# Sliding-window attention and a SMELU feed-forward network: from two stages over DRAM to one interleaved stream with transposed two-head scores

## The chip, the cores and the metric

The kernel runs on one core of one Trainium2 chip. The metric is the device time of one execution in microseconds (us). The runs of one kernel lie between 0.2% and 1.1% apart, lowest to highest. The engines are PE (matmul; weight loads counted apart), DVE (vector), ACT (activation), POOL (which here also issues most transfers) and SP. In the traces of this case each works through its own instructions in program order; run y2 below rests on this. PE leaves its results in PSUM, and the copy that takes one from there to SBUF, where the other tiles lie, is called an eviction.

## The reference

Attention over batch 8, 8 heads, 576 positions and head size 64, in which a query sees the keys at most 32 positions away; then a two-layer network on the 4608 tokens (512 to 2048 to 512) with the SMELU activation.

```
scores = q @ k.T / 8                       # per batch and head
attn   = softmax(where(|i - j| <= 32, scores, -1e9))
x      = (attn @ v), heads side by side     # 4608 x 512
h      = x @ w_in                           # 4608 x 2048
g      = h if h >= 1, 0 if h <= -1, else (h + 1)**2 / 4
out    = g @ w_out                          # 4608 x 512, fp32
```

## The kernel before

Attention goes head by head and by blocks of 128 queries. Scores have queries on the partitions, so the probabilities must be transposed on PE, in up to two chunks, before they meet v. Each chunk of v is a transfer of its own, and x goes out to DRAM, transposed.

```
for qs in qb_starts:                                    # 5 blocks per head
    nc.tensor.matmul(sc[:nq, :nk], qT[:, ds(qs, nq)], kT[:, ds(ks, nk)], ...)
    nc.vector.scalar_tensor_tensor(scs[:nq, :nk], sc[:nq, :nk], 0.125, mask[:nq, :nk], ...)
    nc.scalar.activation(pr[:nq, :nk], scs[:nq, :nk], AF.Exp, accum_out=sm[:nq])
    ...                                                 # reciprocal, scaling
    for ci in range(nchunk):
        nc.tensor.transpose(prT[:cw, :nq], pr[:nq, ds(ci * 128, cw)], ident[:nq, :nq])
        nc.scalar.copy(prTs[:cw, :nq], prT[:cw, :nq])
        nc.gpsimd.dma_start(out=vch[:cw], in_=v[b, h, ds(ks + ci * 128, cw), :])
        nc.tensor.matmul(ot[:, :nq], vch[:cw], prTs[:cw, :nq], ...)
    nc.scalar.copy(osb[:, :nq], ot[:, :nq])
    nc.gpsimd.dma_start(out=xT[ds(h * D, D), ds(b * S + qs, nq)], in_=osb[:, :nq])
```

The network follows when all of x is in DRAM. Its activation takes four DVE passes and one on ACT for each of 144 tiles of 128 x 512:

```
nc.vector.tensor_scalar(t1, hp, 1.0, 0.0, op0=ALU.add, op1=ALU.add)
nc.vector.tensor_scalar(t1, t1, 0.0, 2.0, op0=ALU.max, op1=ALU.min)
nc.scalar.activation(t2, t1, AF.Square, scale=0.5)
nc.vector.tensor_scalar(t1, hp, -1.0, 0.0, op0=ALU.add, op1=ALU.max)
nc.vector.tensor_add(gT[:, f, :], t2, t1)
```

The softmax here doesn't subtract the row's maximum and nothing guards it: scores larger than these inputs give would overflow.

## Time and profile before

The kernel before takes 1139.3 us (median). Its profile has two stages with different limits: attention (about 780 us), in which POOL is full of transfer issues, and the network (about 360 us), in which DVE is full of the activation's passes. The lines, and how each is read, are in the prediction. One digit of the busy map is the busy share of a slice in tenths; a group's line has the total of its busy time, the mean duration in ns, and after the bar the idle time just before its instructions with what ended it.

### The profile page before, as it was taken

Reading aid. Unit: us, or ns where it says so; the run is one execution under the profiler, and the core shown is the slowest. Engines: PE = TensorE matmul, PEld = TensorE weight load, DVE = VectorE, ACT = ScalarE, POOL = GpSimd, SP = SyncE. Lnnn points to the kernel's source line nnn. Section 1 sums busy time; section 2 is a strip of 40 time slices with the busy share of each in tenths; the row PEclk is TensorE's granted clock in tenths of the full one; section 3 lists DMA queues with packets and bytes.
Section 4 is the critical chain, followed back from the end, with each engine's and each line's share of the span. In section 5 each row is a group of like instructions: output and inputs, shape, how many; then the busy total and the mean of one; then the engine's idle time right before and its main releaser. Section 6 shows DMA issues by size and latency. Waiting matters only on the chain.

```text
span 1139.6 us, 13067 instructions
## 1 busy us (share of the span) xinstructions
PE 727.5 (64%) x2920; PEld 294.0 (26%) x2944; DVE 516.2 (45%) x1538; ACT 489.3 (43%) x2037; POOL 737.8 (65%) x1275
## 2 busy tenths in 40 slices
PE   3566656565654455555655655566888888888883
PEld 1222222222221122222222222222233232332321
DVE  1232222222222122222222222233999999999995
ACT  3545545454553345444454444543233323332332
POOL 6999999999998689899998998875001100110000
PEclk9999999999999999999999999999999999999998
DMA  6334434343435533333343333221001100110101
GB/s 92 30 29 32 31 29 31 30 30 29 31 28 65 73 43 30 28 28 30 27 31 27 30 30 26 23 20 13 20 37 55 56 19 38 55 56 19 38 37 38
DMA packets 158399, 40.24 MB, mean 35 GB/s; under 512 B 147184, under 2 KB 154352, under 8 KB 158320
## 3 DMA queue, kind: packets, MB, share of 16 engines
q0 software_dynamic: 158320, 39.40, 30.7%
q8 instruction: 23, 0.38, 0.1%
q14 instruction: 56, 0.46, 0.1%
HBM read 45.61 MB, written 14.16 MB: 52 GB/s over the span
## 4 chain that ended last, share of the span: by engine, by line
issue 40%; POOL 29%; DMA 16%; PE 8%; ACT 5%; DVE 2%; POOLq 0%; ACTq 0%; DVEq 0%
POOL vch L100 12%; DMA vch<-in_v_dram 11%; POOL nat L65 8%; POOL xT L105 7%; DMA nat<-in_q_dram 3%; PE ot L101 3%; PE prT L96 3%; ACT prTs L98 2%; ACT pr L86 2%; POOL out_dram L142 2%; PE sc L80 1%; DMA w_out<-in_moe_w_out_dram 1%; DVE scs L83 1%; PE tp L67 1%; ACT osb L104 1%
## 5 line engine op out<-in xcount | busy, mean ns | idle before, releaser
L100 POOL DMA_DIRECT2D vch<-in_v_dram x576 | 313.2, 547 | 31.9 <-PE ot L101 22.6
L89 DVE RECIPROCAL rs<-sm 128x1 f32<-128x1 f32 (+1 forms) x320 | 51.8, 162 | 546.2 <-ACT pr L86 546.1
L101 PE MATMUL ot<-prTs,vch 128*64 128x128 bf16 (+3 forms) x576 | 174.6, 307 | 101.8 <-DMA vch<-in_v_dram 96.9
L96 PE MATMUL prT<-ident,pr 128*128 128x128 bf16 (+3 forms) x576 | 154.8, 272 | 99.0 <-ACT prTs L98 91.9
L98 ACT COPY prTs<-prT 128x128 bf16<-128x128 bf16 (+3 forms) x576 | 142.8, 252 | 118.8 <-PE ot L101 115.0
L105 POOL DMA_DIRECT2D xT<-osb x320 | 174.5, 545 | 24.0 <-ACT prTs L98 12.9
L132 ACT ACTIVATE t<-t 128x512 f32<-128x512 f32 x144 | 90.7, 630 | 213.4 <-DVE t L130 213.4
L126 PE MATMUL hp<-xc,w_in 128*128 128x512 bf16 x563 | 147.9, 382 | 51.1 <-DVE t L133 50.4
L101 PEld LDWEIGHTS <-vch 128*64 128x64 bf16 (+3 forms) x576 | 72.4, 126 | 310.5 <-DMA vch<-in_v_dram 272.1
L138 PE MATMUL op<-w_out,gT 128*128 128x512 bf16 x565 | 147.9, 381 | 5.4 <-DVE gT L134 4.4
L80 PE MATMUL sc<-kT,qT 64*128 64x192 bf16 (+2 forms) x320 | 96.4, 304 | 81.5 <-DVE scs L83 73.4
L86 ACT ACTIVATE pr<-scs 128x192 bf16<-128x192 f32 (+2 forms) x320 | 109.3, 342 | 69.9 <-PE prT L96 62.0
L104 ACT CAST osb<-ot 64x128 bf16<-64x128 f32 (+1 forms) x320 | 78.1, 244 | 126.6 <-PE ot L101 115.6
L67 PE MATMUL tp<-ident,nat 128*128 128x128 bf16 (+1 forms) x320 | 86.7, 277 | 61.1 <-DMA nat<-in_q_dram 30.2
L65 POOL DMA_DIRECT2D nat<-in_q_dram x160 | 113.7, 711 | 15.6 <-DMA xT<-osb 10.9
L142 POOL DMA_DIRECT2D out_dram<-osb x36 | 19.5, 544 | 154.4 <-ACT osb L141 154.4
L65 POOL DMA_DIRECT2D nat<-in_k_dram x160 | 113.6, 711 | 8.0 <-PE tp L67 5.8
L121 POOL DMA_DIRECT2D xc<-xT x9 | 7.0, 776 | 160.2 <-PE hp L126 160.2
L129 DVE TENSOR_SCALAR t<-hp 128x512 f32<-128x512 f32 x144 | 99.6, 692 | 24.1 <-PE hp L126 9.1
L134 DVE TENSOR_TENSOR gT<-t,t 128x512 bf16<-128x512 f32 x144 | 98.6, 684 | 0.0
L133 DVE TENSOR_SCALAR t<-hp 128x512 f32<-128x512 f32 x144 | 98.1, 681 | 0.2 <-ACT t L132 0.2
L96 PEld LDWEIGHTS <-pr 128*128 128x128 bf16 (+3 forms) x576 | 69.9, 121 | 99.9 <-issue 60.3
(29 smaller groups left out, 582.0 us busy)
## 6 DMA issues: line engine op xcount, KB each, us to landing
out_dram<-osb POOLq DMA_DIRECT2D x36, 256.0 KB, 2.3
xc<-xT POOLq DMA_DIRECT2D x9, 512.0 KB, 4.3
nat<-in_k_dram POOLq DMA_DIRECT2D x128, 32.0 KB, 2.4
vch<-in_v_dram POOLq DMA_DIRECT2D x256, 16.0 KB, 2.1
nat<-in_q_dram POOLq DMA_DIRECT2D x128, 32.0 KB, 2.4
xT<-osb POOLq DMA_DIRECT2D x256, 16.0 KB, 1.8
vch<-in_v_dram POOLq DMA_DIRECT2D x192, 8.0 KB, 2.0
w_in<-in_moe_w_in_dram POOLq DMA_DIRECT2D x1, 2048.0 KB, 12.8
```

The costliest lines, as they stand in the source:

```text
L65: nc.gpsimd.dma_start(out=nat[:cw], in_=src[b, ds(2 * hp, 2), ds(cs, cw), :].rearrange("h s d -> s h d"))
L80: nc.tensor.matmul(sc[:nq, :nk], qT[:, ds(qs, nq)], kT[:, ds(ks, nk)], start=True, stop=True)
L86: nc.scalar.activation(pr[:nq, :nk], scs[:nq, :nk], AF.Exp, accum_out=sm[:nq])
L96: nc.tensor.transpose(prT[:cw, :nq], pr[:nq, ds(ci * 128, cw)], ident[:nq, :nq])
L98: nc.scalar.copy(prTs[:cw, :nq], prT[:cw, :nq])
L100: nc.gpsimd.dma_start(out=vch[:cw], in_=v[b, h, ds(ks + ci * 128, cw), :])
L101: nc.tensor.matmul(ot[:, :nq], vch[:cw], prTs[:cw, :nq], start=(ci == 0), stop=(ci == nchunk - 1))
L105: nc.gpsimd.dma_start(out=xT[ds(h * D, D), ds(b * S + qs, nq)], in_=osb[:, :nq])
L126: nc.tensor.matmul(hp, w_in[:, kk, ds(f * 128, 128)], xc[:, kk, :], start=(kk == 0), stop=(kk == 3))
L129: nc.vector.tensor_scalar(t1, hp, 1.0, 0.0, op0=ALU.add, op1=ALU.add)
L134: nc.vector.tensor_add(gT[:, f, :], t2, t1)
L138: nc.tensor.matmul(op, gT[:, f, ds(tt * 128, 128)], w_out[:, f, :], start=(f == 0), stop=(f == 15))
```

## The change

Its intent is to remove both limits at once. Attention and network become one stream of slots, in which every engine has some of each. Scores are computed transposed, keys on the partitions: a chunk of 64 keys of two heads, interleaved (partition 2s + h), is one weight tile of 128 columns, so no transpose of probabilities is needed. x stays on the chip. q, k and v come in few large transfers; because of their layout (position 9p + j on partition p), the transposed q and k must be spread over their rows when they leave PSUM. The SMELU is rewritten as max(h, -1) + (clamp(h, -1, 1)/2 - 1/2)^2, three passes.

The core of the diff, cut:

```diff
+    def tpose(m, t):                        # 5 or 4 transposes, then the eviction
+            if t < 2:                       # q, on DVE
+                nc.vector.tensor_copy(
+                    qT[m].rearrange("d g (p j) -> d j g p", j=NC)[:, j0:j1],
+                    ps[:, :n].rearrange("d j (g p) -> d j g p", g=2))
+            else:                           # k, on ACT, for 2 heads x 2 pairs
+                        nc.scalar.copy(
+                            kz[...][r].rearrange("d (p j t) -> d t p j", j=NC, t=2)[:, h, :, j0:j1],
+                            ps[r, :n].rearrange("d j (g p) -> d g p j", g=2)[:, g])
...
+            nc.tensor.matmul(ps[:, off:off + q1 - q0], kz[...][:, 128 * c:128 * c + 128],
+                             qT[m][:, gg, q0:q1], start=True, stop=True)
...
+            nc.scalar.activation(pt[i][:, seg], ps[:, :off], AF.Exp, scale=D ** -0.5)
+            nc.gpsimd.tensor_mul(pt[i][:, seg], pt[i][:, seg], maskp[:, seg])
...
+    for a in range(-1, OFF + 16 * (NBLK + 1)):      # the slots
+        if stt:
+            stt()                                    # final pass of the slot before
+            stt = None
+            ... 4 matmuls of the first product into hp ...
+            nc.vector.tensor_scalar(c1, hp, -1.0, 1.0, op0=ALU.max, op1=ALU.min)
+        ... normalisation, scores, exp ...
+            nc.scalar.activation(s1, c1, AF.Square, scale=0.5, bias=-0.5)
+            def stt(hp=hp, s1=s1, blk=blk, f=f):
+                nc.vector.scalar_tensor_tensor(gT[blk][:, f], hp, -1.0, s1, op0=ALU.max, op1=ALU.add)
+        ... 4 matmuls of the second product into op; after the last of 16 a copy on ACT, a store on SP ...
+        ... regrouping, transposes and evictions, or values and denominators ...
```

## The prediction

> **What bounds the kernel now.** I read the busy map of the page first, to see the stages.
> ```profile
> DVE  1232222222222122222222222233999999999995
> POOL 6999999999998689899998998875001100110000
> PEclk9999999999999999999999999999999999999998
> DMA  6334434343435533333343333221001100110101
> ```
> Each digit is a slice of 28.5 us. There are two kernels one after the other: attention for 27 slices (about 780 us) with POOL full, then the MoE for 13 (about 360 us) with DVE full. The TensorE clock is full throughout. The view of stages gives the busy time of each engine inside both:
> ```profile
> 30.00:340.00 310.00, 185.14 (x742) 79.01 (x741) 78.47 (x384) 160.04 (x764) 297.28 (x507) 1.00 0.40 30
> 800.00:1100.00 300.00, 251.40 (x1010) 89.85 (x1029) 285.90 (x514) 97.53 (x161) 22.72 (x39) 1.00 0.12 41
> ```
> The columns are PE, weight loads, DVE, ACT, POOL, then clock, DMA share, GB/s. POOL is busy 297 of 310 us, DVE 286 of 300 us. The chain that ended last agrees for attention: its first entries are
> ```profile
> POOL vch L100 12%; DMA vch<-in_v_dram 11%; POOL nat L65 8%; POOL xT L105 7%; DMA nat<-in_q_dram 3%; PE ot L101 3%; PE prT L96 3%; ACT prTs L98 2%; ACT pr L86 2%; POOL out_dram L142 2%; PE sc L80 1%; DMA w_out<-in_moe_w_out_dram 1%; DVE scs L83 1%; PE tp L67 1%; ACT osb L104 1%
> ```
> The groups, by form (busy us, mean ns), say what fills them:
> ```profile
> L100 POOL DMA_DIRECT2D vch<-in_v_dram x576 | 313.2, 547 | 31.9 <-PE ot L101 22.6 <-PE tp L67 4.8 <-PE prT L96 3.0
> L105 POOL DMA_DIRECT2D xT<-osb x320 | 174.5, 545 | 24.0 <-ACT prTs L98 12.9 <-ACT osb L104 7.6 <-ACT qT L68 2.8
> L129 DVE TENSOR_SCALAR t<-hp 128x512 f32<-128x512 f32 x144 | 99.6, 692 | 24.1 <-PE hp L126 9.1
> L134 DVE TENSOR_TENSOR gT<-t,t 128x512 bf16<-128x512 f32 x144 | 98.6, 684 | 0.0
> L132 ACT ACTIVATE t<-t 128x512 f32<-128x512 f32 x144 | 90.7, 630 | 213.4 <-DVE t L130 213.4
> L130 DVE TENSOR_SCALAR t<-t 128x512 f32<-128x512 f32 x144 | 60.4, 419 | 0.0
> L141 ACT COPY osb<-op 128x512 f32<-128x512 f32 x36 | 20.2, 586 | 17.9 <-DMA out_dram<-osb 13.1 <-PE op L138 4.8
> ```
> Attention: 1,216 issues (576 of v, 320 of x, 320 of q and k at 711 ns) = 313 + 175 + 227 = 715 us of POOL. MoE: four DVE passes, 0.692 + 0.419 + 0.681 + 0.684 = 2.48 us per feature tile, times 144 = 357 us. PE is not at its limit anywhere. What a matmul costs in a stream comes from the timeline:
> ```profile
> 906.92 1.02 PE L126 MATMUL hp<-xc,w_in 128*128 128x512 bf16 x4 [0.79 <-DVE t L133]
> 907.78 1.46 PE L138 MATMUL op<-w_out,gT 128*128 128x512 bf16 x6
> 303.31 0.29 PE L67 MATMUL tp<-ident,nat 128*128 128x128 bf16 x1
> 303.39 0.31 PE L96 MATMUL prT<-ident,pr 128*128 128x128 bf16 x1
> ```
> One lasts 0.38 us, but six take 1.46: (1.46 - 0.38)/5 = 0.216 us each. Two independent ones of 128 columns start 0.08 us apart.
>
> **What the Trainium skill says.** (1) "TensorE: Matmul & The Clock Gate", section "Back-to-back issue gap": 216 ns at N=512, and some 81 ns at N=128 with its weight load. Both agree with the lines above. (2) "VectorE: DVE Perf Modes", section on the TRN2 errata: (N+151)/0.96 ns for a one-per-cycle vector operation, which gives 691 ns at 512 (trace 692, 684); ACT (172+N)/1.2 from PSUM and (224+N)/1.2 from SBUF, 570 and 613 ns at 512 (trace 586, 630, 3% more). I use them for new widths. (3) "GPSIMD Engine Reference", section 3.1: a two-input POOL operation of 2048 elements takes 4497 ns. The trace has no such operation; estimate from that page for 352 to 384 elements: 0.9 us.
>
> **The change part by part.**
> Loads: q and k of four heads in 4 issues of 64 x 2 runs, v of a pair in 2 issues. x and the probabilities no longer move. 64 + 64 + 2 issues on POOL instead of 1,216, and out goes to SP. At 0.57 us per q/k issue (that of 128 runs) and about 0.85 per v issue (576 runs; estimate from 547 and 711 ns for 128 and 256), that is 91 us. POOL gets 96 mask multiplications at 0.9 = 86 us. Total some 180 us instead of 738.
> MoE: three passes, two on DVE (0.69 each from PSUM) and the square on ACT (0.63).
> Scores come out transposed, so the 576 probability transposes and their copies go; a 64-key chunk of two heads meets 96 or 128 queries, nine chunks per pair in groups of 352, 352 and 384 columns.
> The stream has slots: attention runs from slot 0 to 136 (four slots per head pair, first scores at 9), the first MoE products in slots 29 to 172, the second in 45 to 188. Engines keep program order, so a slot costs about its busiest engine. Per full slot:
> - PE: 8 matmuls x 0.216 = 1.73; per pair 9 scores, 9 transposes, 10 value products at 0.08 and 4 denominators at 0.115 = 2.70, a quarter of it 0.67. Sum 2.40.
> - DVE: 2 x 0.69 = 1.38; per eight slots 2 regroupings (0.6 each, estimate), q evictions of 640 and 512 elements (0.82 + 0.69) and 4 normalisations of 288 (0.46) = 4.55, an eighth 0.57. Sum 1.95.
> - ACT: 0.63 + a quarter of 0.586; per pair three exps (1.38), two Ln and Exp pairs (1.62), half of eight k evictions (1.53) = 4.53, a quarter 1.13. Sum 1.91.
> - POOL: per pair 3 x 0.9 + 2 x 0.85 + 2 x 0.57 = 5.5, a quarter 1.4.
> So PE becomes the bound at 2.40. Single PSUM buffers for scores, numerator, denominator and transposes cost little if a consumer finishes within the next slot; by my walk through the eight slot kinds the tightest, the exp after a k eviction, has some 0.4 us to spare. I take 2.5.
>
> Start: a transfer of POOL waits for the one eight issues before (the order of instructions shows these waits), and the first mask multiplications stand behind both weights in POOL's queue. Before, w_in took
> ```profile
> w_in<-in_moe_w_in_dram POOLq DMA_DIRECT2D x1, 2048.0 KB, 12.8
> ```
> and w_out 15.7 us. The page counts 147,184 packets under 512 B, nearly all in some 750 us of attention, so 61,000 in the 310 us above; at a DMA share of 0.40 that is 0.40 x 16 x 310 / 61,000 = 32 ns each. A v issue (576 such packets) then holds the 16 engines 1.15 us; a q/k issue of 147 KB at w_in's rate 0.7 us. To the landing of w_out: 16 x 0.7 + 16 x 1.15 + 10 + 10 + latency = about 53 us, when the third pair's masks (slot 17) can run.
>
> | slots | us each | sum | clock |
> |---|---|---|---|
> | to 16 | - | 53 | 53 |
> | 17-28, attention only (POOL 1.4 and latencies) | 1.65 | 20 | 73 |
> | 29-44, first product only (DVE 1.95) | 2.1 | 34 | 107 |
> | 45-136, full | 2.5 | 230 | 337 |
> | 137-172, MoE only (PE 1.73) | 1.76 | 63 | 400 |
> | 173-188, second product (4 x 0.216) | 0.87 | 14 | 414 |
> | last copy and store | - | 4 | 418 |
>
> **The rivals.**
> (A) ACT sets the full slots. For: slots with k evictions hold 2.6 to 2.9 us of ACT work, and these evictions read PSUM with a long stride, of which the trace has no example. At twice their estimate ACT has 2.3 us per slot, unevenly, and a late exp stalls the next scores: slot 2.75, total 441.
> (B) The waits between engines set it: scores, exp, mask, values, logarithm, product in a row through single buffers, as in attention before, where only the sum of "issue" and transfers explained the pace. Slot 3.2, total 482. Against: no link needs its answer within its own slot.
> (C) The start is hidden better, or small matmuls stream at 56 ns: slot 2.3, start 40: total 387.
> (D) The stream is DMA-bound: per pair 2 x 1.15 + 2 x 0.7 = 3.7 us of engines against 10 us of slots. Unlikely.
>
> **Range and chances.** The centre is 418; C and A give the nearer ends, and unknown operations (strided evictions, POOL product) mostly lengthen, so 393 to 470. Only a failure of the whole interleave would bring it near 1139: POOL's 715 and DVE's 357 us in series are gone whatever else happens. Faster 0.99.
>
> **What would show it.** PE should be densest from about 107 us on, 8 or 9 tenths and more, with hp and op matmuls as the last link of the chain, and DVE, ACT near 75 to 80% there. POOL's first mask product should stand behind weight transfers until about 40 us, with a gap to about 53. A full stretch of 16 slots should take 40 us, one of the MoE tail 28. Wrong if in 107 to 337 us PE waits for exp (A) or for a chain through all engines (B), if k evictions take over 0.5 us, or if the DVE evictions into strided places take over 0.9.

## The result, and the profile after

The changed kernel takes **473.3 us** (median of 4 runs, 471.9 to 474.0) against 1139.3, a ratio of 0.416 [0.415, 0.416]. A ratio is the mean time of one kernel's runs over that of the other's in the same rounds, so not quite the ratio of the medians quoted. The forecast said 418 within 393 to 470: the direction was clear, the size is 3 us outside the range and 55 us from the centre.

The busy map of the changed kernel (slices of 11.8 us) shows one stage instead of two, in which PE is the densest but not full:
```profile
PE   0135458567979787878787879787878999798976
DVE  5633556868777777777777777777776666666610
ACT  1057557575767666666666666666667743333320
POOL 8647586262717171717171726232223200000000
```
The chain of waits that ended last names PE only for parts of it. Evictions of k on ACT (L164), the clamp (L260) and the square (L268) stand beside PE:
```profile
PE op L277 18%; PE hp L257 13%; ACT kz L164 11%; DVE c L260 10%; ACT s L268 6%; ACT osb L281 4%; DVE qT L157 4%; DVE gT L271 3%; PE tp L152 3%; ACT pt L188 2%; PE nm L206 2%; PE sc L180 1%; POOL vz L96 1%; DVE xT L217 1%; PE dn L197 1%
```
The groups by form (busy us, mean ns) show the sizes of the new instructions:
```profile
L271 DVE SCALAR_TENSOR_TENSOR gT<-hp,s 128x512 bf16<-128x512 f32 x144 | 104.3, 724 | 104.4 <-ACT s L268 104.4
L260 DVE TENSOR_SCALAR c<-hp 128x512 f32<-128x512 f32 x144 | 97.8, 679 | 3.5 <-PE hp L257 3.5
L189 POOL TENSOR_TENSOR pt<-pt,maskp 128x352 bf16<-128x352 bf16 x64 | 55.1, 862 | 149.6 <-ACT pt L188 149.2
L157 DVE COPY qT<-tp 128x640 bf16<-128x640 bf16 x16 | 47.6, 2975 | 7.5 <-PE tp L152 7.5
L157 DVE COPY qT<-tp 128x512 bf16<-128x512 bf16 x16 | 38.7, 2416 | 2.1 <-PE tp L152 2.1
L164 ACT COPY kz<-tp 64x320 bf16<-64x320 bf16 x64 | 41.1, 743 | 30.4 <-PE tp L152 30.2
```
The clamp, the final pass and the mask product have the sizes that the prediction took (0.69 and 0.9 us). The q evictions (L157) take 2.98 and 2.42 us where it took 0.82 and 0.69; the k evictions (L164) 0.74 where its formula for ACT gives 0.41.

The timeline shows what these long pieces do. First a q eviction in the full part of the stream (start us, length us, engine, line; in brackets the idle time before and what ended it; lines between these are left out, here and in the next two views):
```profile
241.72 0.68 DVE L260 TENSOR_SCALAR c<-hp 128x512 f32<-128x512 f32 x1
242.44 0.63 ACT L268 ACTIVATE s<-c 128x512 f32<-128x512 f32 x1 [0.58 <-DVE c L260]
242.68 2.99 DVE L157 COPY qT<-tp 128x640 bf16<-128x640 bf16 x1
245.28 0.91 DVE L271 SCALAR_TENSOR_TENSOR gT<-hp,s 128x512 bf16<-128x512 f32 x1
246.09 0.70 DVE L260 TENSOR_SCALAR c<-hp 128x512 f32<-128x512 f32 x1
246.82 0.63 ACT L268 ACTIVATE s<-c 128x512 f32<-128x512 f32 x1 [2.92 <-DVE c L260]
```
While DVE works on the eviction, ACT does what else it has (two pieces, not shown) and then runs out of work: its next square waits 2.92 us for the clamp. Then a k eviction, a little later:
```profile
302.25 2.59 ACT L164 COPY kz<-tp 64x320 bf16<-64x320 bf16 x4
302.52 0.68 DVE L260 TENSOR_SCALAR c<-hp 128x512 f32<-128x512 f32 x1
305.23 0.62 ACT L268 ACTIVATE s<-c 128x512 f32<-128x512 f32 x1
305.89 0.69 DVE L271 SCALAR_TENSOR_TENSOR gT<-hp,s 128x512 bf16<-128x512 f32 x1 [2.68 <-ACT s L268]
```
Now DVE waits, 2.68 us, for a square that stands behind the k evictions on ACT. Each engine waits out the other's long piece. Even in the last part, with no attention left, the two take turns; here is one round of it:
```profile
446.44 0.69 DVE L271 SCALAR_TENSOR_TENSOR gT<-hp,s 128x512 bf16<-128x512 f32 x1 [0.76 <-ACT s L268]
447.05 0.68 DVE L260 TENSOR_SCALAR c<-hp 128x512 f32<-128x512 f32 x1
447.82 0.63 ACT L268 ACTIVATE s<-c 128x512 f32<-128x512 f32 x1 [1.41 <-DVE c L260]
448.48 0.69 DVE L271 SCALAR_TENSOR_TENSOR gT<-hp,s 128x512 bf16<-128x512 f32 x1 [0.76 <-ACT s L268]
```
A slot lasts 448.48 - 446.44 = 2.04 us, the sum of clamp, square and final pass with their hand-offs, though its PE work is 1.73 us. That is one loop: in program order the final pass of a slot stands before the clamp of the next one on DVE, the clamp feeds the square on ACT, and the square feeds the final pass.

Read off the first instructions of each part, the stages compare so with the prediction:

| slots | predicted us | measured us | how measured |
|---|---|---|---|
| to 28 | 73 | 69.5 | first matmul of the first product |
| 29 to 44 | 34 | 46.7 | first matmul of the second product at 116.2 |
| 45 to 172 | 293 | 334.8 | its last part begins at 451.0 |
| 173 to 188 | 14 | 16.6 | last matmul ends at 467.7 |
| end | 4 | 3.8 | span 471.4 |

The start came out near the prediction. These POOL lines show the first mask products at 37 us (40 was predicted) and the wait for w_out's landing, at 49 us (53):
```profile
37.31 2.52 POOL L189 TENSOR_TENSOR pt<-pt,maskp 128x352 bf16<-128x352 bf16 x3
49.19 0.60 POOL L89 DMA_DIRECT2D kn<-in_k_dram  x1 [1.56 <-DMA w_out<-in_moe_w_out_dram]
```
The loss lies in slots 29 to 172. In the full part eight slots recur every 23.3 us, 2.92 us each instead of 2.5. A look at slots 29 to 44 gives a first hint: they cost the same 2.92 us (46.7/16) although they lack the second product, which speaks against PE's work as the limit. It is no more than a hint, for the granted clock was low in this part (0.74 between 100 and 120 us, 0.98 from 120 to 200). The clock does not explain the whole: of the four runs the one with the lowest mean clock, 0.956, was the fastest, 471.9 us.

### The profile page after: what moved, and what is told of

Its sections match the earlier page's. It is cut to its first block, busy times and chain, and to the rows that moved or that the text cites. A ratio compares the mean times of both kernels' runs of the same rounds, so it can differ in the third digit from the quotient of the medians.

```text
span 471.4 us, 6061 instructions
## 1 busy us (share of the span) xinstructions
PE 347.5 (74%) x2176; PEld 183.1 (39%) x2176; DVE 311.1 (66%) x441; ACT 268.9 (57%) x533; POOL 175.0 (37%) x236
## 4 chain that ended last, share of the span: by engine, by line
PE 39%; ACT 23%; DVE 19%; issue 15%; POOL 2%; ACTq 0%; DVEq 0%; POOLq 0%
PE op L277 18%; PE hp L257 13%; ACT kz L164 11%; DVE c L260 10%; ACT s L268 6%; ACT osb L281 4%; DVE qT L157 4%; DVE gT L271 3%; PE tp L152 3%; ACT pt L188 2%; PE nm L206 2%; PE sc L180 1%; POOL vz L96 1%; DVE xT L217 1%; PE dn L197 1%
## 5 line engine op out<-in xcount | busy, mean ns | idle before, releaser
L271 DVE SCALAR_TENSOR_TENSOR gT<-hp,s 128x512 bf16<-128x512 f32 x144 | 104.3, 724 | 104.4 <-ACT s L268 104.4
L268 ACT ACTIVATE s<-c 128x512 f32<-128x512 f32 x144 | 90.5, 628 | 137.7 <-DVE c L260 137.2
L257 PE MATMUL hp<-xT,w_in 128*128 128x512 bf16 x576 | 153.8, 390 | 2.0 <-DVE xT L217 1.8
L189 POOL TENSOR_TENSOR pt<-pt,maskp 128x352 bf16<-128x352 bf16 (+1 forms) x96 | 84.3, 881 | 185.5 <-ACT pt L188 185.0
L260 DVE TENSOR_SCALAR c<-hp 128x512 f32<-128x512 f32 x144 | 97.8, 679 | 3.5 <-PE hp L257 3.5
L164 ACT COPY kz<-tp 64x320 bf16<-64x320 bf16 (+1 forms) x128 | 77.4, 711 | 31.2 <-PE tp L152 30.9
L157 DVE COPY qT<-tp 128x640 bf16<-128x640 bf16 (+1 forms) x32 | 86.3, 2696 | 9.7 <-PE tp L152 9.7
L277 PEld LDWEIGHTS <-gT 128*128 128x128 bf16 x576 | 54.6, 98 | 93.8 <-issue 44.2
L257 PEld LDWEIGHTS <-w_in 128*128 128x128 bf16 x576 | 53.3, 100 | 45.8 <-issue 4.6
L96 POOL DMA_DIRECT2D vz<-in_v_dram x64 | 50.0, 789 | 11.2 <-DMA w_in<-in_moe_w_in_dram 10.4
L281 ACT COPY osb<-op 128x512 f32<-128x512 f32 x36 | 20.5, 569 | 14.9 <-PE op L277 14.9
L206 PEld LDWEIGHTS <-vz 128*128 128x128 bf16 x320 | 23.3, 107 | 9.5 <-issue 5.9
```

Of the source, the lines that this page charges most:

```text
L96: nc.gpsimd.dma_start(out=vz[i % 8][h:128:2, :, 64 * h:64 * h + 64], in_=v[b, 2 * hp + h].rearrange("(c p) d -> p c d", p=64))
L157: nc.vector.tensor_copy(qT[m].rearrange("d g (p j) -> d j g p", j=NC)[:, j0:j1], ps[:, :n].rearrange("d j (g p) -> d j g p", g=2))
L164: nc.scalar.copy(kz[2 * (m % 2) + g][r].rearrange("d (p j t) -> d t p j", j=NC, t=2)[:, h, :, j0:j1], ps[r, :n].rearrange("d j (g p) -> d ...
L189: nc.gpsimd.tensor_mul(pt[i][:, seg], pt[i][:, seg], maskp[:, seg])
L206: nc.tensor.matmul(nm[:, q0 - lo:q1 - lo], vz[i % 8][:, c], pt[i][:, pcol(c, q0):pcol(c, q1)], start=n == 0, stop=n == len(parts) - 1, ski ...
L257: nc.tensor.matmul(hp, w_in[:, kk, 128 * f:128 * f + 128], xT[:, kk, TB * blk:TB * blk + TB], start=kk == 0, stop=kk == 3)
```

## The experiments

The theories were these; the first three stood before the first four runs, the fourth came out of their results. (1) The evictions of q on DVE are larger than assumed and set the pace. (2) Those of k on ACT do. (3) The chain of waits through single PSUM buffers does. (4) The loop of clamp, square and final pass ties DVE and ACT together, so that the long pieces of both add up.

Twelve kernels ran. The median of the changed kernel, 473.3 us, is the base of all differences. The slot lengths of the full part come from the number of matmuls in a stretch of the trace (16 per slot) or from the recurring period.

| run | what was altered | us | full slot, us |
|---|---|---|---|
| - | the change | 473.3 | 2.92 |
| x2_q_flat | q eviction written contiguously (wrong order) | 425.0 | 2.48 |
| x3_k_flat | k eviction written contiguously (wrong order) | 447.4 | 2.61 to 2.84 |
| x4_qk_flat | both | 397.3 | 2.22 |
| y1_q_order | q eviction with turned loops | 427.9 | 2.49 |
| y2_stt_late | loop opened | 434.2 | 2.60 |
| y3_q_late | turned loops, loop opened | 403.5 | 2.34 |
| y4_q_late_bal | the same, a quarter of k on DVE | 421.6 | 2.51 |
| z1_flat_late | both contiguous (wrong order), loop opened | 383.9 | 2.21 |
| z2_k_word_late | y3 with k as whole words | 386.6 | 2.21 |
| z3_ps_o2 | second buffer for the second product | 465.8 | 2.91 |

**A caution on correctness.** The comparison with the reference passed even for the four kernels that put q or k in the wrong order. With these inputs a pass therefore does not vouch for the handling of q and k, only for the rest; that holds for the change itself too. The reference draws q and k at 0.1 of a unit normal, so the scores are about 0.01 (an estimate: 8 x 0.01 / 8), and softmax weights that are nearly equal would hide a wrong order.

### The eviction by itself: x1_evict_forms

A kernel that only transposes once and then repeats eight forms of one eviction, six times each, on DVE and on ACT.

```diff
+        # 1: both sides contiguous
+        # 2: as in the kernel for q: contiguous read, writes 18 B apart
+        # 3: reads 256 B apart, writes in runs of 5
+        # 4: contiguous read, writes in runs of 5
+        # 5: reads 256 B apart, contiguous write
+        # 6: contiguous read, writes 4 B apart (512 elements)
+        # 7: as in the kernel for k: 64 partitions, reads 256 B apart, writes 4 B apart in runs of 5
+        # 8: as 7, read run by run
```

> Output wrong on purpose; only durations matter. Each of eight forms of one PSUM eviction runs six times alone, on DVE and on ACT, 640 bf16 elements per partition (512 in form 6, 320 on 64 partitions in forms 7 and 8). If writes 18 B apart are what makes the q eviction slow, form 2 takes about 2.98 us on DVE, and forms 1 and 5 (contiguous writes) 0.8 us; form 4 (runs of five) lies between. If it is the reading or the four-dimensional pattern, forms 3 and 5 (reads 256 B apart) are slow and form 2 alone is fast. On ACT form 7 should repeat the kernel's 0.74 us; if its long-stride read is the cost, form 8 drops to about 0.41 us, if its spread writes are, form 8 stays at 0.74.

The groups by form (L54 is form 1, L58 form 2, L62 form 3, L78 form 7):
```profile
L58 ACT COPY a_w<-ps 128x640 bf16<-128x640 bf16 x6 | 17.7, 2949 | 0.2
L58 DVE COPY v_w<-ps 128x640 bf16<-128x640 bf16 x6 | 17.7, 2944 | 0.2
L62 DVE COPY v_r256w<-ps 128x640 bf16<-128x640 bf16 x6 | 5.1, 858 | 0.2
L78 ACT COPY a_k<-ps 64x320 bf16<-64x320 bf16 x6 | 4.3, 711 | 0.2
L54 ACT COPY a_flat<-ps 128x640 bf16<-128x640 bf16 x6 | 4.2, 692 | 0.2
L54 DVE COPY v_flat<-ps 128x640 bf16<-128x640 bf16 x6 | 2.9, 492 | 2.3 <-PE ps L41 2.1
```
It is the writes. With reads contiguous and writes 18 B apart, 640 elements take 2.94 us on either engine, against 0.49 (DVE) and 0.69 (ACT) with both sides contiguous: per element (2944 - 492)/640 = 3.8 ns more on DVE. The long-stride read costs DVE 0.33 us (form 5: 0.82) and ACT nothing (form 5: 0.69, as form 1). Writing runs of five elements takes 0.70 us on DVE with a contiguous read (form 4) and 0.86 with the long-stride one (form 3). The expectation had form 1 at 0.8 us, and form 4 between that and 2.98: contiguous copies, and so runs of five, are cheaper on DVE than it said. For k, form 8 (another way of reading) took 0.72 us, as form 7 did: again the reading isn't the cost. Writes 4 B apart over a long row cost something too (form 6: 512 elements took 0.72 us on DVE and 0.73 on ACT, where 640 contiguous ones took 0.49 and 0.69); in short runs with jumps between, 320 elements take as long (form 7).

The Trainium skill states the matter on its page "SBUF — State Buffer", section "Specifications (TRN2)": lines of 16 bytes, at least two hits in a line for full bandwidth, a penalty for each access that crosses to a new line. Writes 18 B apart cross to a new line every time. The trace agrees, and puts a number to it that the page does not give. No run varied the distance, so that 16 bytes is the limit is not shown here. The prediction overlooked this.

### One eviction at a time, and both: x2_q_flat, x3_k_flat, x4_qk_flat

```diff
 # x2, x4: q
-                    qT[m].rearrange("d g (p j) -> d j g p", j=NC)[:, j0:j1],
-                    ps[:, :n].rearrange("d j (g p) -> d j g p", g=2))
+                    qT[m].rearrange("d g s -> d (g s)")[:, 128 * j0:128 * j1],
+                    ps[:, :n].rearrange("d j x -> d (j x)"))
 # x3, x4: k
-    kz[...][r].rearrange("d (p j t) -> d t p j", j=NC, t=2)[:, h, :, j0:j1],
-    ps[r, :n].rearrange("d j (g p) -> d g p j", g=2)[:, g])
+    kz[...][r].rearrange("d (t j p) -> d t j p", j=NC, t=2)[:, h, j0:j1],
+    ps[r, :n].rearrange("d j (g p) -> d g j p", g=2)[:, g])
```

> Output wrong on purpose: the q eviction on DVE is written contiguously, in the wrong order, all else as in the change. Theory 1 (the q eviction, 2.98 and 2.42 us where 0.82 and 0.69 were assumed, sets the pace of the full slots through DVE): DVE loses 3.9 us per eight slots, the eight-slot period falls from 23.3 to about 20 us, over 13.5 periods 45 us, and the start gains 2 to 4: 425 us, within 10. Theory 2 (the k evictions on ACT set it): over 460. Theory 3 (the chain of waits through single buffers sets it): over 460 as well.

Measured: **425.0 us** (ratio to the kernel before 0.373 [0.372, 0.374]), 48 less than the change, as theory 1 expected; theories 2 and 3 had it over 460.

> Output wrong on purpose: only the k evictions on ACT are written contiguously, read in runs of 64. Theory 1: under 12 us gained, 461 or more. Theory 2: ACT loses some 2.6 us per eight slots (0.74 and 0.68 to about 0.41 and 0.36 us, eight of them), 13.5 periods: 35 us, so 438. Theory 3: over 460.

Measured: **447.4 us** (0.393 [0.391, 0.395]), 26 less. Theory 1 alone is refuted by this: it allowed 12. So k evictions matter as well, though less than theory 2 had it (438). Theory 3 (over 460) fails here too. This kernel's runs had the lowest granted clocks (0.94 to 0.97; 0.91 in some stretches up to 200 us), so 26 may be too little: eight slots took up to 22.7 us across such a stretch, and 21.2, or 2.65 each, outside it.

> Output wrong on purpose: both evictions contiguous. This gives the evictions the durations that the prediction assumed, so if only their size was wrong, the time is the predicted 418 us within 8, with full slots at 2.5 us (20 us per eight). If theory 3 holds, it stays above 450, and full slots at 2.75 us or more.

Measured: **397.3 us** (0.349 [0.348, 0.351]), 76 less, about the sum of the two gains (48 + 26), and outside the expected 410 to 426. If DVE alone or ACT alone had set the pace, shortening the other engine would have gained nothing, so the additive result is what led to theory 4. It does not prove it: slots with a q eviction bound by DVE and slots with a k eviction bound by ACT, without any loop, would add up as well. And 397 is less than the predicted 418. The view of stages tells why (PE, weight loads, DVE, ACT, POOL, clock, DMA share, GB/s):
```profile
97.00:200.00 103.00, 103.00 (x743) 57.88 (x742) 77.70 (x140) 81.28 (x188) 64.46 (x83) 1.00 0.60 81
```
PE is busy for the whole 103 us. It runs 743 matmuls in that time, 743/16 = 46.4 slots, 2.22 us each, where the prediction's sum for PE was 2.40 and its slot 2.5. The reason is the small matmuls: in the timeline of the change, five transposes in a row take
```profile
240.75 0.44 PE L152 MATMUL tp<-ident,qj 128*128 128x128 bf16 x5
```
and one alone about 0.24 us, so they start (0.44 - 0.24)/4 = 0.05 us apart, not 0.08.

### Undoing the cost of q rightly: y1_q_order

```diff
-                    qT[m].rearrange("d g (p j) -> d j g p", j=NC)[:, j0:j1],
-                    ps[:, :n].rearrange("d j (g p) -> d j g p", g=2))
+                    qT[m].rearrange("d g (p j) -> d g p j", j=NC)[:, :, :, j0:j1],
+                    ps[:, :n].rearrange("d j (g p) -> d g p j", g=2))
```

> Right output by construction: the same q eviction with the loops turned, so that it reads PSUM 256 B apart and writes runs of five or four (forms alone: 0.86 us for 640 elements instead of 2.94). DVE then loses 3.8 us per eight slots, nearly what the contiguous write took away (4.5), so 425 plus a few: 428 us, within 6. If the writes 18 B apart were not the cause but something else that the contiguous write also removed, it stays above 450.

Measured: **427.9 us** (0.376 [0.374, 0.377]). The evictions now take 0.82 and 0.72 us, nearly the sizes that the prediction had taken (0.82 and 0.69). The same elements go to the same places; only the order of the walk has changed, and it is worth 45 us.

### Opening the loop: y2_stt_late

```diff
-        if stt:
-            stt()
-            stt = None
+        late, stt = stt, None
         ...
             nc.vector.tensor_scalar(c1, hp, -1.0, 1.0, op0=ALU.max, op1=ALU.min)
+        if late:
+            late()
```

> Right output. The change with one thing moved: on DVE the clamp of a slot stands ahead of the final pass of the slot before. Theory 4 (clamp, square and final pass form a closed loop over DVE and ACT, so that each engine waits out the other's long evictions and the two add up): the loop opens, the eight-slot period falls from 23.3 us to the busier engine's sum, 19.5 to 20.5, and MoE-only slots from 2.04 to 1.76: 473 - 38 - 8, about 427 us, within 10. If occupancy of DVE alone set the pace (19.4 of 23.3 us busy plus waits that the eviction itself makes), the order changes little: over 460.

Measured: **434.2 us** (0.382 [0.381, 0.382]), 39 less than the change. No instruction was removed or shortened: the q evictions still take 2.97 us. The eight-slot period fell from 23.3 to 20.8 us (19.5 to 20.5 was expected), a slot without attention from 2.04 to about 1.8. This supports theory 4 and refutes the view that the sum of one engine's work set the pace of the change; nor would slots that are bound by one engine each, without a loop, gain from a change of order alone. The same stretch of the full part, in the change and then here (columns as above):
```profile
120.00:200.00 80.00, 66.49 (x452) 35.66 (x451) 60.40 (x84) 53.94 (x110) 39.83 (x53) 0.98 0.47 63
120.00:200.00 80.00, 71.37 (x494) 38.37 (x494) 67.83 (x93) 58.89 (x123) 40.50 (x53) 1.00 0.52 72
```
DVE is now busy 67.8 of 80 us, 17.6 of the 20.8 us of a period; in the change it was the same 17.6 of 23.3. (The 19.4 of the expectation is the sum of durations, which overlap a little in the trace.)

### Both: y3_q_late

The edits of y1 and y2 together.

> Right output: both of the above. Theory 4: per slot DVE 1.93, ACT 2.25 (its k evictions still slow), PE 2.22, all side by side: full slots at 2.3, MoE-only at 1.76: about 391 us, within 10, less than with both evictions contiguous and the loop closed (397). If the loop does not matter, some 428 us.

Measured: **403.5 us** (0.354 [0.353, 0.355]). This is below either edit alone, as theory 4 had it (428 if the loop does not matter), but the size was missed: 12 us over the 391 expected, outside its range, and not below the 397 of x4 as forecast. Full slots take 2.34 us, and ACT, which still has the slow k evictions, is busy 67.6 of 80 us there; z2 below shows what these cost. The two gains overlap (45 and 39 alone, 70 together).

### A repair that failed: y4_q_late_bal

```diff
-                        nc.scalar.copy(
+                        (nc.vector.tensor_copy if h == 1 and g == 1 else nc.scalar.copy)(
```

> Right output: as the one before, and one of four k evictions goes to DVE, so ACT falls to 2.08 and DVE rises to 2.11 per slot. If ACT is then what holds PE up, PE sets the pace at 2.22: about 384 us, within 8. If not, the same as the one before within 3 us.

Measured: **421.6 us** (0.370 [0.369, 0.371]), 18 slower than y3, against both expectations. The waits (who waited for whom: us in total, times, longest us) name a new one:
```profile
DVE kz L164 <- ACT kz L164: 62.0, 31, 2.8
```
The copy that was moved to DVE writes a tile into which ACT has just written, and reads the same PSUM tile, so DVE stands until ACT's copies are done, up to 2.8 us, and the clamps stand behind it. By this reading, moving work to a free engine had tied the two engines together again. Which of the two shared tiles forces the wait was not tested.

### Contiguous and open: z1_flat_late

The edits of x4 and y2 together.

> Output wrong on purpose (q and k in the wrong order): both evictions contiguous as before (397 us) and the final pass moved behind the next clamp. Theory 4 says that the closed loop of clamp, square and final pass (0.68 + 0.63 + 0.69 and hand-offs = 2.04 us) is what paces the slots without attention, 36 of them: they fall to PE's 1.73 to 1.82, 8 to 11 us in all; full slots stay at PE's 2.22. So 387 us, within 6. If the loop does not pace them: 397.

Measured: **383.9 us** (0.337 [0.336, 0.339]), 13 less than with the loop closed (397.3) at the same full slot, 2.21 us (8 to 11 less were expected). So the gain lies outside the full slots; slots without attention now take about 1.8 us (89 matmuls in 20 us, 8 per slot), not 2.04 (x4: 158 in 40 us, 2.03). This fits theory 4 there too.

### Whole words for k: z2_k_word_late and z4_word_check

Each 4-byte word of the k tile holds one key and one zero. So a bf16 key widened to fp32, or its 16 bits widened as an integer, fills the word in one write.

```diff
+                        wi, wo = ((mybir.dt.uint16, mybir.dt.uint32), (BF, FP))[h]
                         nc.scalar.copy(
-                            kz[...][r].rearrange("d (p j t) -> d t p j", j=NC, t=2)[:, h, :, j0:j1],
-                            ps[r, :n].rearrange("d j (g p) -> d g p j", g=2)[:, g])
+                            kz[...][r].bitcast(wo).rearrange("d (p j) -> d p j", j=NC)[:, :, j0:j1],
+                            ps[r, :n].bitcast(wi).rearrange("d j (g p) -> d g p j", g=2)[:, g])
```

> Right output: the version with turned q loops and the opened loop (403.5 us), and k evicted as whole 4-byte words: head 0 as 16-bit integers widened to 32, head 1 as bf16 widened to fp32, so that each word holds one key and one zero. If two-byte writes 4 B apart in short runs are what makes a k eviction 0.74 us, it falls to about 0.42 us, ACT to some 1.9 us per slot, and the time to PE's pace: 390 us, within 7. If the short runs or the long-stride read cost as much with whole words, the eviction stays above 0.65 and the time at 400 or more.

Measured: **386.6 us** (0.339 [0.338, 0.340]), as expected and 17 less than y3. The evictions fell to 0.45 us for 320 elements, with the same jumps and the same reads, so the two-byte writes 4 B apart were the cost of k. PE is again busy throughout the full part, at 2.21 us per slot.

```diff
+    dif, dmx = kz - kzo, ...                   # kzo: evicted as in the change
+    fw = max over a row of (kz - kzo)**2 * 1e8
+    ff = min(1, max over a row of (kz - kzf)**2 * 1e8)   # kzf: contiguous, wrong order
-                nc.scalar.copy(osb, op)
+                nc.vector.tensor_scalar(osb, op, ff, fw, op0=ALU.mult, op1=ALU.add)
```

(The first three lines are shortened to what they compute.)

> A test of correctness, since the comparison with the reference passed with q and k in a wrong order. The kernel of whole-word evictions also evicts k of the first eight heads as the change does and in the contiguous wrong order, compares all three on the chip, adds the squared difference to the first times 1e8 to the output, and multiplies the output by one if the contiguous one differs, by zero if not. So it passes only if whole words equal the change's keys and the wrong order is told apart. Expected: correct. The time says nothing.

Measured: **wrong**, relative error 14. The test was written so that it passes only if the keys agree almost to the last bit, so by this test they don't. It was not tried on a kernel that ought to pass, so a fault of the test itself is not excluded. Whether the integer or the fp32 half is inexact, and by how much a key is off, was not settled. The time of z2 counts as evidence of what the eviction costs, but z2 is not offered as an equal kernel; the fastest version that puts q and k in the same places as the change, by construction, is y3, at 403.5 us.

### Single buffers: z3_ps_o2

```diff
-    ps_h = ctx.enter_context(tc.tile_pool(name="ps_h", bufs=3, space=bass.MemoryType.PSUM))
-    ps_o = ctx.enter_context(tc.tile_pool(name="ps_o", bufs=1, space=bass.MemoryType.PSUM))
+    ps_h = ctx.enter_context(tc.tile_pool(name="ps_h", bufs=2, space=bass.MemoryType.PSUM))
+    ps_o = ctx.enter_context(tc.tile_pool(name="ps_o", bufs=2, space=bass.MemoryType.PSUM))
```

> Right output: the change with a second PSUM buffer for the second product, taken from the first product (two instead of three). Theory 3 (single buffers: PE stands 36 us for the copy that empties the one buffer of the second product): that wait goes, some 30 us gained, 443. Theory 4: the copy is late only because the loop is, PE then waits elsewhere instead (for the first product's buffers or the scores), and only the 16 last slots gain, 2 to 3 us: 468, above 460.

Measured: **465.8 us** (0.409 [0.408, 0.410]), 7 less. In the change PE's largest wait was
```profile
PE op L277 <- ACT osb L281: 36.2, 34, 2.0
```
With two buffers it is gone from the head of the list, and in its place stands
```profile
PE hp L257 <- DVE gT L271: 55.9, 72, 2.7
```
PE now waits for the buffers of the first product, which the late final pass frees, and eight slots still recur every 23.3 us. The test had to take its buffer from the first product, so by itself it doesn't tell what a ninth buffer would give. The trace of y2, which kept the buffers as in the change, settles more:
```profile
PE op L277 <- ACT osb L281: 12.0, 32, 1.1
```
With the loop open, two thirds of the wait for this one buffer are gone. So theory 3 is refuted as the main cause for this buffer: the wait that it named was mostly a symptom. The other single buffers (scores, numerator, denominator, transposes) were not tested.

## Why the prediction was wrong

**What held.** POOL's and DVE's old limits fell as forecast. The start was right within 4 us, and the mask products did stand behind weight transfers; the number is in part luck, for with short evictions the same slots took 63.2 us (x4), 10 less than predicted. The sizes of the clamp, the final pass, the mask product, the exps and the normalisation were right within a few per cent. The part of the sum called "29-44" came out at 34.0 us in x4, as predicted, once the evictions were short.

**The step that failed first** is the term "q evictions of 640 and 512 elements (0.82 + 0.69)" of DVE's sum, and with it "half of eight k evictions (1.53)" of ACT's. The q term measured 2.98 + 2.42 us. The k term measured (4 x 0.743 + 4 x 0.679)/2 = 2.84 us. The prediction had said that unknown strided evictions would "mostly lengthen", yet put them into the sum at the price of one element per cycle, strides or not. Two of its own signs of being wrong came true by this: k evictions over 0.5 us, and strided DVE evictions over 0.9. Making both contiguous is worth 76 us (x4); giving q the assumed size is worth 45 (y1). The cause is the pattern of the writes (18 B apart for q; two bytes at a time, 4 B apart in short runs, for k), not the long-stride read which rival A had suspected (x1, z2).

**The second step that failed** is the argument against rival B, "no link needs its answer within its own slot". The final pass of a slot must be done before DVE starts the next clamp, and it needs the square of that clamp's predecessor on ACT. This closed loop made the long pieces of DVE and ACT add up, which is why neither engine was full (DVE 60.4 of 80 us in the stretch from 120 to 200 us) and both evictions mattered. Opening it is worth 39 us with everything else as it was (y2). The same loop falsified the line "137-172, MoE only (PE 1.73)": those slots took 2.04 us. Rival B said 482 us, near the measured 473, and waits between engines were indeed a part; but as it was put, through single PSUM buffers, it was not the main cause where it was tested (z3, y2).

**Errors on the other side** hid a part of this. PE's 2.40 was too high: small matmuls start 0.05 us apart, a full slot of PE is 2.22 us (x4). The extra 0.1 us that the prediction added was not needed. Over 92 full slots that is (2.5 - 2.22) x 92 = 26 us in the prediction's favour, and the start was 4 us shorter (10 in x4). Had the evictions had their assumed sizes, the same loop would still have been there, and the kernel would have taken some 400 us (397 in x4, whose q evictions are even shorter, and y1 is 3 us above x2), below the centre but within the range.

**The range** failed because it treated the slow eviction and the waits between engines as rivals, one to take the place of the other. But each made the other expensive: the loop is harmless while no engine has a long piece (x4 to z1: 13 us) and cost 39 when both have one (y2).

## What to carry to other kernels

Price an eviction by the distance between its writes, and if two walks reach the same places, take the one that writes in runs: a turned loop saved 45 us here. In a software pipeline over in-order engines, look for a closed loop (A feeds B, B feeds a later instruction of A that stands before A's next start); move the consumer one step later before counting the engines' sums as parallel. A wait that the profile names for a buffer can be a symptom: give it a second buffer, and see whether the wait moves. And before a pass is trusted, try whether the inputs can tell a wrong order at all.

## What the Trainium skill lacked or had wrong

- "SBUF — State Buffer", section "Specifications (TRN2)": it has the rule of 16-byte lines but neither the size of the penalty nor that it strikes DVE and ACT alike as they write. These runs: 640 bf16 elements written 18 B apart took 2.944 us on DVE and 2.949 us on ACT, against 0.492 and 0.692 us written contiguously. Nor does it tell of two-byte writes 4 B apart in runs of five, where most lines get their two hits: 0.711 us for 320 elements on ACT, but 0.450 us as whole words with the same jumps.
- "TensorE: Matmul & The Clock Gate", section "Back-to-back issue gap": its some 81 ns per matmul with a weight load at N=128 was too high here; five transposes with their weight loads started 0.05 us apart, near the page's figure for an isolated gap, some 56 ns. At N=512 the same section has some 131 ns for a stream, and calls 216 ns, which the prediction took from the page, the isolated gap; in the kernel before, six in a row started 0.216 us apart.
- No page that I read warns that in-order engines can close a loop through program order alone. These runs: 473.3 us closed, 434.2 us open, with the same instructions.
